# SwiGLU feed-forward on one core: six feature chunks in place of four are projected ahead of the regular loop

## Chip, core and metric

The kernel runs on one core of a Trainium2 chip. The metric is the device time of one execution in microseconds, lower is better. A run's profile gives the span between its first and last instruction, which is a little shorter than that time.

## What is computed

```python
B, S, D, F = 1, 2048, 640, 1536          # all bf16
def reference(x, w_gate, w_up, w_down):  # x [1,2048,640], w_gate, w_up [640,1536], w_down [1536,640]
    g = silu(x @ w_gate)
    u = x @ w_up
    return (g * u) @ w_down
```

## The kernel before

The 2048 rows of x are handled in four blocks of 512 (`sb`). TensorE needs x transposed, with the 640 features on partitions; `xT` holds it as five K steps (`kd`) of 128 features. The 1536 hidden features are twelve chunks of 128 (`fc`). For each block and chunk, five matmuls over `kd` accumulate the gate sum `pg` and five the up sum `pu`, each [128 features x 512 rows] of f32, that is one PSUM bank. `gate` (L210 to L217) then runs ScalarE (silu of `pg` into `sg`, L214) and VectorE (`sg` times `pu` into `aT`, L215). When a block's twelve chunks are done, the down projection runs: the last 128 output columns transposed (`po_t`, L261) and the first 512 in four groups of 128 rows (`po_a`, L291). ScalarE copies results out, SP and ACT issue the output DMAs. VectorE also computes the last four rows of the hidden layer by dot products (`row_dots`, L147) beside the matmuls, on transposed copies of the weights.

PSUM has eight banks, handed out by tag: "gu" has four, "po_a" two, "po_b" two. In the regular loop `pg` and `pu` of a chunk both come from "gu".

The first block starts differently, since nothing is loaded yet. The order of DMA issues sets what arrives when:

- the first 128 rows of x on SP's queue, the next 128 on ACT's (L86);
- five slices of the gate weights, one for each K step, 128 partitions x `EARLY` x 128 columns, by turns on SP's queue (K steps 0, 2, 4) and ACT's (1, 3) (L115);
- on SP, the crossbar copy `turn_x`, which brings rows 256 to 511 of x into `xT` transposed by the DMA engines (L105);
- on SP, the up weights of the early chunks two chunks at a time, then gate and up weights of the rest by `W_CHUNKS` (L83), then w_down (L125), the next block's crossbar copy, the broadcast rows and the transposed weights.

The order of SP's instructions is pinned at the end (`keep_order`, L314). A DMA issue waits until the DMA that used its semaphore last, eight DMAs earlier, has landed.

`head` (L219) is TensorE's work at the start. It issues 18 matmuls on a tile of ones (`warm`, L176), whose sums are not used; then it transposes the first 256 rows of x on TensorE into PSUM tiles `pt`, two K steps in a "po_a" bank that ScalarE copies to `xT` and three in a "po_b" bank that VectorE copies (L185, L190). Then come the gate sums of `EARLY` chunks side by side, K step by K step: K step 0 in two pieces of 128 rows, K steps 1 to 4 for the first 256 rows, then all five for the second 256 rows, which need the crossbar copy. Only then come the up sums of these chunks one after the other, with `gate` behind each. PE's and ACT's order is pinned as written (L241, L242). The loop at L245 skips the chunks that `head` has done.

Of the kernel before, what the change touches and what calls it, by code (L numbers as in the profile page):

```python
# [10 lines left out]
def _body(  # L11
# [9 lines left out]
    P = nc.NUM_PARTITIONS  # L21
    f32 = mybir.dt.float32
# [12 lines left out]
    S_BLK = 512  # L35
# [6 lines left out]
    T = 4  # L42
    WT_STEP = 4
    ROW_J = 0
    EARLY = 4
    W_CHUNKS = [(4, 8), (8, 12)]
    assert D % P == 0 and F % P == 0 and S % S_BLK == 0 and D > DA and SUB == 4

    consts = ctx.enter_context(tc.tile_pool(name="consts", bufs=1))
# [2 lines left out]
    psum = ctx.enter_context(  # L52
        tc.tile_pool(name="psum", bufs=2, space=bass.MemoryType.PSUM)
    )
# [24 lines left out]
    def wslice(a, b):  # L79
        return slice(a * P, b * P)  # L80

    def load_w(eng, dst, src, a, b):
        eng.dma_start(out=dst[:, :, wslice(a, b)], in_=src[:, :, wslice(a, b)])  # L83
# [14 lines left out]
    def keep_order(engine):  # L98

        traced = [i for i in nc.cur_bb.bb.instructions if i.engine == engine]  # L100
        for a, b in zip(traced, traced[1:]):
            issue_order(a, b)
# [10 lines left out]
    for kd in range(KD):  # L113
        eng = (nc.sync, nc.scalar)[kd % 2]
        eng.dma_start(  # L115
            out=wg_sb[:, kd, wslice(0, EARLY)], in_=wg_v[:, kd, wslice(0, EARLY)]
        )
    turn_x(HALF, S_BLK)
    nc.scalar.activation(silu_first[:], ones[:, 0:1], ACT.Silu)  # L119
    for a in range(0, EARLY, 2):  # L120
        load_w(nc.sync, wu_sb, wu_v, a, a + 2)
    for a, b in W_CHUNKS:
        load_w(nc.sync, wg_sb, wg_v, a, b)
# [50 lines left out]
    def warm(n):  # L174
        for _ in range(n):
            nc.tensor.matmul(  # L176
                pw[:, 0:P], lhsT=ones[:], rhs=ones[:], start=True, stop=True
            )

    def transpose_chunk(c, parts):  # L180
        c_sl = slice(c * P, (c + 1) * P)
        for copy, tag, k0, k1 in parts:
            pt = psum.tile([P, k1 - k0, P], bf16, tag=tag, name="pt")
            for kd in range(k0, k1):
                nc.tensor.transpose(  # L185
                    out=pt[:, kd - k0, :],
                    in_=x_sb[:, c, kd * P : (kd + 1) * P],
                    identity=ident[:],
                )
            copy(out=xT[:, k0:k1, c_sl], in_=pt[:])  # L190

    def proj_step(ps, w_sb, fc, sb, c0, c1, kd):
        nc.tensor.matmul(  # L193
            ps[:, c0:c1],
            lhsT=w_sb[:, kd, fc * P : (fc + 1) * P],
            rhs=xT[:, kd, sb * S_BLK + c0 : sb * S_BLK + c1],
            start=(kd == 0 and c0 in (0, HALF)),
            stop=(kd == KD - 1),
        )

    def proj(ps, w_sb, fc, sb, c0, c1):
        for kd in range(KD):
            proj_step(ps, w_sb, fc, sb, c0, c1, kd)

    def gu_tiles():
        pg = psum.tile([P, S_BLK], f32, tag="gu", name="pg", bufs=4)
        pu = psum.tile([P, S_BLK], f32, tag="gu", name="pu", bufs=4)
        return pg, pu

    def gate(pg, pu, sb, fc, n_s):  # L210

        s0 = sb * S_BLK
        sg = work.tile([P, S_BLK], f32, name="sg")
        nc.scalar.activation(sg[:, 0:n_s], pg[:, 0:n_s], ACT.Silu)  # L214
        nc.vector.tensor_tensor(  # L215
            out=aT[:, fc, s0 : s0 + n_s], in0=sg[:, 0:n_s], in1=pu[:, 0:n_s], op=ALU.mult
        )  # L217

    def head():  # L219
        dve, act = nc.vector.tensor_copy, nc.scalar.copy  # L220
        split = [(act, "po_a", 0, 2), (dve, "po_b", 2, KD)]
        pgs = [
            psum.tile([P, S_BLK], f32, tag="gu", name="pg", bufs=4)
            for _ in range(EARLY)
        ]
        warm(N_WARM)
        for c in range(HALF // P):
            transpose_chunk(c, split)

        steps = [(0, 0, P), (0, P, HALF)]  # L230
        steps += [(kd, 0, HALF) for kd in range(1, KD)]
        steps += [(kd, HALF, S_BLK) for kd in range(KD)]
        for kd, c0, c1 in steps:
            for fc in range(EARLY):
                proj_step(pgs[fc], wg_sb, fc, 0, c0, c1, kd)

        for fc in range(EARLY):
            pu = psum.tile([P, S_BLK], f32, tag=("po_a", "po_b")[fc % 2], name="pu")
            proj(pu, wu_sb, fc, 0, 0, S_BLK)
            gate(pgs[fc], pu, 0, fc, S_BLK)  # L240
        keep_order(mybir.EngineType.PE)  # L241
        keep_order(mybir.EngineType.Activation)  # L242

    head()
    for sb in range(NSB):  # L245
        n_s = S_BLK if sb < NSB - 1 else S_BLK - T
        for fc in range(KF):
            if sb == 0 and fc < EARLY:
                continue
            pg, pu = gu_tiles()  # L250
# [134 lines left out]
def kernel(tc, *args):  # L385
    _body(tc, *args)
    tc.close()
    tc.compile()
    _trim(tc.nc)
# [30 lines left out]
```

## Time and profile before

| | |
|---|---|
| median of three runs | 163.66 us (163.44 to 163.76) |
| the profiled execution, and its span | 163.73 us, 162.4 us |
| TensorE (PE) busy | 159.4 us, 98% of the span |
| VectorE (DVE), ScalarE (ACT) busy | 111.1 us, 42.6 us |
| DMA moved | 15.86 MB |
| gate matmuls (L193, `pg`) | 60.1 us |
| up matmuls (L193, `pu`) | 59.0 us |
| down projection (L291, L261) | 42.4 us and 10.3 us |

PE is the matmul unit, PEld its weight loads, which run beside it; SPq and ACTq are DMA issues from the SP and ACT queues. A group's line gives engine, operation, output and input tiles, shapes and count, then busy time, mean ns of one, and the idle time of the engine ahead of it with what ended it. A matmul's duration contains its drain, which overlaps the next one; the distance between two starts is what a stream of them costs. A DMA's time runs from issue to landing. Some matmul records are missing from the trace.

### The profile page before, as it was taken

How to read it: one execution, taken by the hardware profiler on the slowest of the kernel's cores; microseconds unless marked ns; L12 is line 12 of the kernel's file. 1: busy time of each engine (PE TensorE's matmuls, PEld its weight loads, DVE VectorE, ACT ScalarE, POOL GpSimd, SP SyncE). 2: the span in 40 equal slices, each digit the busy share in tenths (PEclk: the TensorE clock that was granted, in tenths of full speed). 3: DMA queues.
4: the chain of work that ended last, by engine and by line, in shares of the span. 5: the costliest groups of instructions: out<-in, count | busy, mean ns of one | idle time of the engine just before them, and what ended most of it. 6: DMA issues, size and time to landing. Idle time of an engine off the chain costs nothing.

```text
span 162.4 us, 2129 instructions
## 1 busy us (share of the span) xinstructions
PE 159.4 (98%) x796; PEld 78.0 (48%) x808; DVE 111.1 (68%) x250; ACT 42.6 (26%) x74; POOL 0.6 (0%) x6
## 2 busy tenths in 40 slices
PE   8999999999999999999999999999999999999995
PEld 8754444444444444444444444444444444445454
DVE  1024333499559999979919999979964999993101
ACT  5051222112232222221222322221214222222121
POOL 1000000000000000000000000000000000000000
PEclk9999999999999999999999999999999999999999
DMA  7999999995169997003110000000421000000212
GB/s 215 259 339 350 362 184 250 228 231 88 53 125 178 217 176 145 4 0 34 65 65 0 0 4 2 0 0 0 65 67 34 0 0 0 0 0 4 44 45 73
DMA packets 41961, 15.86 MB, mean 98 GB/s; under 512 B 33504, under 2 KB 41824, under 8 KB 41952
## 3 DMA queue, kind: packets, MB, share of 16 engines
q1 hardware_dynamic: 33440, 14.80, 38.0%
q10 hardware_dynamic: 8512, 0.94, 3.9%
q8 instruction: 6, 0.10, 0.3%
q14 instruction: 3, 0.02, 0.1%
HBM read 6.88 MB, written 2.62 MB: 59 GB/s over the span
## 4 chain that ended last, share of the span: by engine, by line
PE 97%; DMA 2%; issue 0%; DVE 0%
PE pg L193 32%; PE pu L193 32%; PE po_a L291 26%; PE po_t L261 6%; DMA x_sb<-in_x_dram 2%; PE pt L185 1%; DVE ot_b L302 0%
## 5 line engine op out<-in xcount | busy, mean ns | idle before, releaser
L193 PE MATMUL pg<-xT,wg_sb 128*128 128x512 bf16 (+3 forms) x258 | 60.1, 366 | 0.3
L193 PE MATMUL pu<-xT,wu_sb 128*128 128x512 bf16 (+1 forms) x239 | 59.0, 379 | 0.1
L215 DVE TENSOR_TENSOR aT<-sg,pu 128x512 bf16<-128x512 f32 (+1 forms) x48 | 32.8, 683 | 32.9 <-PE pu L193 32.9
L214 ACT ACTIVATE sg<-pg 128x512 f32<-128x512 f32 (+1 forms) x48 | 28.4, 596 | 71.5 <-PE pg L193 67.7
L291 PE MATMUL po_a<-wd_sb,aT 128*128 128x512 bf16 (+4 forms) x224 | 42.4, 348 | 0.2
L147 DVE SCALAR_TENSOR_TENSOR prod<-wgT,x_row 128x640 f32<-128x640 bf16 x48 | 39.4, 821 | 1.1
L147 DVE SCALAR_TENSOR_TENSOR prod<-wuT,x_row 128x640 f32<-128x640 bf16 x48 | 39.4, 822 | 1.0
L193 PEld LDWEIGHTS <-wg_sb 128*128 128x128 bf16 x264 | 26.3, 101 | 26.8 <-DMA wg_sb<-in_w_gate_dram 0.2
L193 PEld LDWEIGHTS <-wu_sb 128*128 128x128 bf16 x240 | 23.5, 98 | 28.0
L291 PEld LDWEIGHTS <-aT 128*128 128x128 bf16 x228 | 20.8, 98 | 21.7
L300 ACT CAST ot<-po_a 128x512 bf16<-128x512 f32 (+2 forms) x17 | 9.5, 560 | 31.8 <-PE po_a L291 20.6
L261 PE MATMUL po_t<-aT,wd_sb 128*128 128x512 bf16 (+1 forms) x47 | 10.3, 365 | 0.1
L261 PEld LDWEIGHTS <-wd_sb 128*128 128x128 bf16 x48 | 4.7, 98 | 5.1
L302 DVE CAST ot_b<-po_a 128x96 bf16<-128x96 f32 (+1 forms) x2 | 0.5, 242 | 9.7 <-PE po_a L291 9.6
L270 ACT CAST ot_t<-po_t 128x512 bf16<-128x512 f32 (+1 forms) x4 | 2.2, 560 | 11.6 <-PE po_t L261 11.6
L147 DVE DVE_READ_ACCUMULATOR prod<-wuT,x_row 128x1 f32 x48 | 3.9, 82 | 0.0
L147 DVE DVE_READ_ACCUMULATOR prod<-wgT,x_row 128x1 f32 x48 | 3.9, 82 | 0.0
L272 DVE STREAM_TRANSPOSE ot_q<-ot_t 128x512 bf16<-128x512 bf16 (+1 forms) x4 | 2.7, 678 | 1.7 <-ACT ot_t L270 1.7
L190 DVE COPY xT<-pt 128x384 bf16<-128x384 bf16 x2 | 0.7, 358 | 3.2 <-PE pt L185 3.2
L176 PE MATMUL pw<-ones 128*128 128x128 bf16 x18 | 2.1, 312 | 0.4 <-DVE ones L109 0.4
L176 PEld LDWEIGHTS <-ones 128*128 128x128 bf16 x18 | 1.8, 146 | 0.4 <-DVE ones L109 0.4
L119 ACT ACT_TABLE_LOAD x1 | 1.3, 1283 | 1.5 <-issue 1.5
(13 smaller groups left out, 4.7 us busy)
## 6 DMA issues: line engine op xcount, KB each, us to landing
wd_sb<-in_w_down_dram SPq DMA_DIRECT2D x1, 1920.0 KB, 14.2
out_dram<-ot SPq DMA_DIRECT2D x15, 128.0 KB, 1.7
wg_sb<-in_w_gate_dram SPq DMA_DIRECT2D x2, 640.0 KB, 8.3
wu_sb<-in_w_up_dram SPq DMA_DIRECT2D x2, 640.0 KB, 8.9
wu_sb<-in_w_up_dram SPq DMA_DIRECT2D x2, 320.0 KB, 5.4
x_row<-in_x_dram SPq DMA_DIRECT2D x1, 640.0 KB, 4.8
wg_sb<-in_w_gate_dram SPq DMA_DIRECT2D x3, 128.0 KB, 3.9
out_dram<-ot_q ACTq DMA_DIRECT2D x12, 32.0 KB, 2.0
```

The lines of the kernel that those rows point to most:

```text
L119: nc.scalar.activation(silu_first[:], ones[:, 0:1], ACT.Silu)
L147: nc.vector.scalar_tensor_tensor(out=prod[:], in0=wT[:, fc, :], scalar=1.0, in1=x_row[:, t, :], op0=ALU.mult, op1=ALU.mult, accum_out=acc[ ...
L176: nc.tensor.matmul(pw[:, 0:P], lhsT=ones[:], rhs=ones[:], start=True, stop=True)
L185: nc.tensor.transpose(out=pt[:, kd - k0, :], in_=x_sb[:, c, kd * P : (kd + 1) * P], identity=ident[:],)
L193: nc.tensor.matmul(ps[:, c0:c1], lhsT=w_sb[:, kd, fc * P : (fc + 1) * P], rhs=xT[:, kd, sb * S_BLK + c0 : sb * S_BLK + c1], start=(kd == 0 ...
L214: nc.scalar.activation(sg[:, 0:n_s], pg[:, 0:n_s], ACT.Silu)
L215: nc.vector.tensor_tensor(out=aT[:, fc, s0 : s0 + n_s], in0=sg[:, 0:n_s], in1=pu[:, 0:n_s], op=ALU.mult)
L261: nc.tensor.matmul(po_t[:], lhsT=wd_sb[:, kf, DA:D], rhs=aT[:, kf, sb * S_BLK : sb * S_BLK + n_t], start=(kf == 0), stop=(kf == KF - 1),)
L270: nc.scalar.copy(ot_t[:], po_t[:])
L272: nc.vector.transpose(out=ot_q[:], in_=ot_t[:])
L291: nc.tensor.matmul(po[:], lhsT=aT[:, kf, s0 : s0 + P], rhs=wd_sb[:, kf, c0:c1], start=(kf == 0), stop=(kf == KF - 1),)
L300: nc.scalar.copy(ot[:], po[:])
```

## The change

`EARLY` becomes 6. The five gate slices ahead of the crossbar copy have 768 columns (192 KB) in place of 512 (128 KB). Three loads of up weights of two chunks each follow it in place of two, and the remaining six chunks are loaded three at a time in place of four. The gate sums of the early chunks take six banks: four of "gu" and the two of "po_a", allocated once the transposes have used these. The early up sums have the two banks of "po_b" in place of taking "po_a" and "po_b" by turns.

```diff
-    EARLY = 4
-    W_CHUNKS = [(4, 8), (8, 12)]
+    EARLY = 6
+    W_CHUNKS = [(6, 9), (9, 12)]
...
         pgs = [
-            psum.tile([P, S_BLK], f32, tag="gu", name="pg", bufs=4)
-            for _ in range(EARLY)
+            psum.tile([P, S_BLK], f32, tag="gu", name="pg", bufs=4) for _ in range(4)
         ]
         warm(N_WARM)
         for c in range(HALF // P):
             transpose_chunk(c, split)
+        pgs += [
+            psum.tile([P, S_BLK], f32, tag="po_a", name="pg") for _ in range(4, EARLY)
+        ]
...
         for fc in range(EARLY):
-            pu = psum.tile([P, S_BLK], f32, tag=("po_a", "po_b")[fc % 2], name="pu")
+            pu = psum.tile([P, S_BLK], f32, tag="po_b", name="pu")
             proj(pu, wu_sb, fc, 0, 0, S_BLK)
             gate(pgs[fc], pu, 0, fc, S_BLK)
```

## The prediction

> **What bounds the kernel now.** The page's first part and its two strips come first.
>
> ```profile
> span 162.4 us, 2129 instructions
> PE 159.4 (98%) x796; PEld 78.0 (48%) x808; DVE 111.1 (68%) x250; ACT 42.6 (26%) x74; POOL 0.6 (0%) x6
> ...
> PE   8999999999999999999999999999999999999995
> ...
> PE pg L193 32%; PE pu L193 32%; PE po_a L291 26%; PE po_t L261 6%; DMA x_sb<-in_x_dram 2%; PE pt L185 1%; DVE ot_b L302 0%
> ```
>
> PE is busy in every slice but the first and the last, and the chain is PE almost alone. A dense stretch cannot be shortened by reordering it: 216 ns separate the starts of two 512-column matmuls, and the change leaves the number of streamed columns as it is. What can move is the head. Second view: busy time by stretches of the first 14 us (stretch, length, then PE busy).
>
> ```profile
> 2.30:2.64 0.34, 0.20 (x2) 0.00 (x1) 0.00 (x0) 0.34 (x1) 0.00 (x0) 1.00 1.18 357
> 2.64:3.68 1.04, 1.04 (x10) 1.04 (x11) 0.29 (x1) 0.81 (x4) 0.00 (x0) 1.00 0.96 318
> 3.68:4.54 0.86, 0.86 (x10) 0.79 (x8) 0.43 (x2) 0.30 (x1) 0.00 (x0) 1.00 1.06 302
> 4.54:4.63 0.09, 0.09 (x2) 0.00 (x1) 0.00 (x0) 0.00 (x0) 0.00 (x0) 1.00 1.56 307
> 4.63:6.30 1.67, 1.67 (x10) 1.19 (x9) 0.00 (x0) 0.00 (x0) 0.00 (x0) 1.00 1.24 234
> 7.22:9.40 2.18, 2.18 (x22) 1.95 (x20) 0.00 (x0) 0.12 (x1) 0.00 (x0) 1.00 1.09 307
> ```
>
> PE starts the x transposes at 2.64, the gate matmuls at 3.68. In 4.54 to 4.63 it starts nothing new (the 0.09 "busy" is the drain of earlier matmuls): the second gate slice is late, as the timeline says.
>
> ```profile
> 3.58 0.90 PEld L193 LDWEIGHTS <-wg_sb 128*128 128x128 bf16 x8
> 4.63 0.13 PEld L193 LDWEIGHTS <-wg_sb 128*128 128x128 bf16 x2 [0.15 <-DMA wg_sb<-in_w_gate_dram]
> ```
>
> Third, the same form of matmul, grouped by form, in 4.64 to 6.0 and in 6.6 to 7.2:
>
> ```profile
> L193 PE MATMUL pg<-xT,wg_sb 128*128 128x256 bf16 x7 | 1.7, 417 | 0.0
> ...
> L193 PE MATMUL pg<-xT,wg_sb 128*128 128x256 bf16 x8 | 1.1, 277 | 0.0
> ```
>
> By their starts they are 213 ns apart until 6.3 us and 109 ns apart from 6.5 on. So PE runs at **half rate until about 6.3**, though PEclk in the page reads full throughout. From 6.5 to its last matmul at 160.4 PE has no gap that is not a missing record (each odd gap is one 216 ns start). Hence the end is set by three things: how long PE idles before 6.3, when the full rate starts, and the column count. DVE, ACT and the tail after 160.4 follow.
>
> Fourth, DMA issues with their time to landing, in the windows 0.5 to 0.6 and 1.8 to 1.9.
>
> ```profile
> wg_sb<-in_w_gate_dram SPq DMA_DIRECT2D x1, 128.0 KB, 2.9
> wg_sb<-in_w_gate_dram ACTq DMA_DIRECT2D x1, 128.0 KB, 4.0
> ...
> wg_sb<-in_w_gate_dram SPq DMA_DIRECT2D x1, 128.0 KB, 4.0
> xT<-in_x_dram SPq DMA_TRANSPOSE x1, 4.8
> ```
>
> With the issue starts (0.46, 0.55, 0.91, 1.03, 1.39, 1.86) the five gate slices kd0 to kd4 land at 3.3, 4.6, 4.8, 5.2 and 5.4, the crossbar copy at 6.7. PE asks for them at 3.58, 4.53, 5.25, 6.10, 6.68 and 7.22. Only kd1 is late; the crossbar copy is 0.5 us early.
>
> **The change, part by part.** *Columns.* Per K step, the gates of chunks 4 and 5 become two 256-column matmuls for one of 512 (at kd0 one 256 is two of 128). At half rate they cost the same (2 x 213 = 427), at full rate 2 x 109 - 216 = 2 ns more; ten pairs: **+0.02 us**. The same columns that were computed later are gone there.
>
> *Slices of 192 KB.* Each gate slice grows by 64 KB (65.5 kB), five by 328 kB. The table above moves 302 to 318 GB/s up to 4.54 and 234 after.
> kd0: 65.5 kB take 0.21 us alone and 0.41 beside as much of kd1 on ACT's queue, so it lands at 3.5 to 3.7. PE asks at 3.58, and a landing took 0.04 us to start PE (4.59 to 4.63): a wait of 0 to 0.2.
> kd1: PE now has 12 matmuls of 128 columns before it, at 107 ns, 3.68 + 1.28 = 4.96. Ahead of its landing are 131 kB more (its own and kd0's) or 197 kB (with kd2's, which runs beside it): 0.43 to 0.65 us at 302 GB/s, 0.84 at 234. It lands at 5.0 to 5.4, and PE starts on it at 5.1 to 5.5. All idle time up to there, kd0's included, is 0.1 to 0.5 us, where it was 0.1. If the longer rows of 1536 bytes move faster, kd1 may land by 4.9 and the 0.1 is gone. So the bounds are -0.1 and +0.4 us of idle time; I take **+0.17**, between the two middle figures less 0.1 (0.11 and 0.22), because most of this traffic flows in the 302 to 318 stretches.
> kd2 (about 5.6), kd3 (6.1) and kd4 (6.5) are asked for at 6.4 and after: no wait.
>
> *What an idle 0.1 us costs.* If the full rate starts at 6.3 whatever happens, PE loses half-rate time and the cost is half: 0.08. If the start moves with the idle time it is all: 0.17. With the 0.02 that is **+0.1 to +0.2**.
>
> *The crossbar copy* stands behind the slices on SP's queue: 328 kB at 302 or 234 GB/s are 1.1 to 1.4 us, so it lands at 7.8 to 8.1. PE now reaches the second half after the rest of kd1 (to about 6.5) and 18 matmuls at 109 ns: 8.5. Hidden with 0.4 us or more, as before; where the gate starts the full rate later, PE comes later still. The up weights land about 1.4 us later (8.7 becomes 10.1) and are asked for 2.2 us later (9.3, plus two gates of 1.08, is 11.5): hidden. Chunk 6's gate weights are asked for at 11.5 + 6 x 1.08 = 18; the same number of bytes, gate and up weights of eight chunks, had landed by 13.6 (issued at 5.70, 7.9 to landing), and those of all twelve by 18.5: hidden. SP issues one DMA more (about 0.5 to 1 us, from the 0.53 and 0.84 of its neighbours), ahead of a long queue; nothing waits for it. wd, the transposed weights and x_row follow with the same total of bytes.
>
> *PSUM.* Gate sums 4 and 5 take the banks of ACT's two x copies. These end at 3.44 and 3.98 (3.07 and 3.60, each 0.37 long); the fifth and sixth matmul start at 3.68 + 4 x 0.107 = 4.11 and 4.21: free. The up sums now share two banks where they had four, so up sum n + 2 waits for the multiplication of n:
>
> ```profile
> 9.40 3.40 PE L193 MATMUL pu<-xT,wu_sb 128*128 128x512 bf16 x14
> 10.76 0.69 DVE L215 TENSOR_TENSOR aT<-sg,pu 128x512 bf16<-128x512 f32 x1 [6.48 <-PE pu L193]
> ```
>
> The first up sum starts at 9.40, its product ends at 11.45, and with 0.05 for the release (the first LDWEIGHTS of the run came 0.05 after DVE's memset) PE is free at 11.50; the third up sum starts at 9.40 + 10 x 0.216 = 11.56. **0.06 us of cover**, four times. If the product came 0.1 us later, each wait would be 0.04 and all six chunks behind PE would shift by some 0.1 in all. Cost: 0, bounds 0 and 0.2. ACT's silus run ahead, limited by the three sg buffers as now (ACT waited 0.63 for DVE once, with the next product 2 us away).
>
> **Sum.** 0.02 + 0.08 to 0.17 + 0 = +0.1 to +0.2. The profiled execution took 163.73 us, 162.4 of span and 1.3 around it; it lies 0.07 above the median of 163.66. I forecast **163.85**, against the median.
>
> **The rivals.**
> *B, the full rate comes much later (slower).* PE was busy from 0.40 to 2.30 without reaching it, idled 0.35, and then needed 2.64 to 6.3, 3.7 us, with a hole of 0.09 inside. If a hole of 0.2 or more starts that count anew, as the 0.35 may have done, then a wait at kd0 alone puts it at 3.85 + 3.7 = 7.5, one at kd1 at 5.2 + 3.7 = 8.9. That is 1.2 to 2.6 us more at half rate, half of it lost: +0.6 to +1.3, **164.3 to 165.0**. It decides once the hole passes something between 0.09 and 0.35 us. For it: the two spells above. Against: one hole of 0.09 did no harm.
> [...]
> *C, no wait at all.* The longer rows move faster and kd1 is in time: -0.1 of idle plus 0.02, **163.55 to 163.65**. For it: 12 matmuls of cover in place of 8. Against: kd1's slowest landing came 1.3 us after kd0's, in traffic that only grows.
> *D, faster.* The hole at 4.54 held the full rate back, and without it the rate starts 0.7 us or more earlier: -0.35 or more, **163.3** and below. For it: the largest price in the head is the 2.64 to 6.3 at half rate, 1.8 us lost. Against: needs C first, and the count after 2.64 can hardly be shorter than the spell of 1.9 us that did not reach it.
> *E, two banks for the up sums bind:* +0.1 to 0.2, **163.75 to 163.85** alone; it hides inside the forecast and has no chance of its own.
>
> **How the numbers follow.** The forecast's case 0.50, B 0.28, C 0.10, D 0.12. About 0.2%, 0.33 us, is what a measurement of this kernel can tell from no change, that is 163.33 to 163.99. The forecast's case holds 163.6 to 164.3 (idle up to +0.4 at full price, a bank wait on top): 0.32 of it within the bound, 0.18 above. C is within, B above, D below. Faster 0.12, same 0.42, slower 0.46. The range is 163.4 to 165.0: all of the forecast's case and C, most of B.
>
> **What would show it.** Waits of LDWEIGHTS on wg_sb in the head: one or two, 0.1 to 0.5 us in all. The 256-column matmuls turn from 417 to about 275 ns: at 6.3 to 6.6 the forecast holds, after 7.3 it is B, before 5.6 D. A wait of PE on the crossbar copy, or of a pu matmul on DVE, would show two of my zeros wrong. If PE has a gap after 12 us, the reading that only the head can move is wrong.

## The result and the profile after

The changed kernel took 164.12 us (median of 22 runs, 163.26 to 164.98), the kernel before 163.53 us (22 runs, 162.99 to 163.82) in the same series: a ratio of 1.0043 with a 95% interval of 1.0029 to 1.0058. The forecast was 163.85 against a median of 163.66, that is +0.19; measured is +0.59, inside the range, on the slower side, and from a place that the forecast had put at zero. The profiled execution of the changed kernel took 164.98 us, the longest of its runs, so what follows shows a larger loss than the median run has.

The page of the changed kernel, first part, chain and two groups (the last two columns of a group: busy time with mean ns, and idle time ahead of it with what ended it):

```profile
span 163.7 us, 2152 instructions
PE 159.2 (97%) x808; PEld 78.9 (48%) x820; DVE 111.1 (68%) x250; ACT 42.5 (26%) x74; POOL 0.6 (0%) x6
...
PE   8999999996999999999999999999999999999995
...
PE 74%; SPq 15%; DMA 5%; DVE 2%; ACTq 2%; issue 1%; ACT 0%; DVEq 0%
...
L293 PE MATMUL po_a<-wd_sb,aT 128*128 128x512 bf16 (+4 forms) x224 | 42.6, 348 | 1.6 <-ACT ot L302 1.4
...
L147 DVE SCALAR_TENSOR_TENSOR prod<-wgT,x_row 128x640 f32<-128x640 bf16 x48 | 39.4, 822 | 2.6 <-DMA wgT<-in_w_gate_dram 1.5
```

PE's strip has a 6 in its tenth slice (36.8 to 40.9 us), in the middle of what was a solid row of nines. The chain, which was PE to 97%, now has 15% of DMA issues on SP and 5% of DMA in it. The two groups name both ends of the new wait: the down projection `po_a` waits 1.4 us for ScalarE's copy `ot`, and VectorE's dot products wait 1.5 us for the transposed gate weights `wgT`. What lies between them shows in the timeline. VectorE of before, 31 to 36 us, and then of after (start, length):

```profile
31.86 0.82 DVE L147 SCALAR_TENSOR_TENSOR prod<-wgT,x_row 128x640 f32<-128x640 bf16 x1
...
34.40 0.71 DVE L272 STREAM_TRANSPOSE ot_q<-ot_t 128x512 bf16<-128x512 bf16 x1
```
```profile
33.15 0.83 DVE L147 SCALAR_TENSOR_TENSOR prod<-wgT,x_row 128x640 f32<-128x640 bf16 x1 [1.48 <-DMA wgT<-in_w_gate_dram]
...
35.63 0.71 DVE L274 STREAM_TRANSPOSE ot_q<-ot_t 128x512 bf16<-128x512 bf16 x1
```

ScalarE, 33 to 41 us, before and after:

```profile
35.14 2.04 ACTq L274 DMA_DIRECT2D out_dram<-ot_q  x4
37.23 0.59 ACT L300 CAST ot<-po_a 128x512 bf16<-128x512 f32 x1 [2.86 <-DVE prod L147]
```
```profile
36.37 2.98 ACTq L276 DMA_DIRECT2D out_dram<-ot_q  x4
39.40 1.07 ACT L302 CAST ot<-po_a 128x512 bf16<-128x512 f32 x2 [5.31 <-DVE prod L147]
```

And PE, 30 to 41 us, before and after:

```profile
33.58 7.72 PE L291 MATMUL po_a<-wd_sb,aT 128*128 128x512 bf16 x35
```
```profile
33.30 5.34 PE L293 MATMUL po_a<-wd_sb,aT 128*128 128x512 bf16 x23
40.03 1.24 PE L293 MATMUL po_a<-wd_sb,aT 128*128 128x512 bf16 x5 [1.39 <-ACT ot L302]
```

Read downwards, it is one queue behind another. VectorE worked in the written order (the third dot product starts at 34.88, the transposition at 35.63): three dot products stand ahead of the transposition `ot_q` of block 0's last 128 output columns, and they start 1.29 us later (33.15 against 31.86). The transposition is 1.23 us later. ScalarE's four output DMAs of `ot_q` wait for it and take 0.94 us longer to issue (one of the four takes 1.50 us). Behind them on ScalarE stands the copy of the first output group: 39.40 against 37.23, 2.17 us later. The groups have two PSUM banks, so PE's third group needs that copy's end. Before, the copy ended at 37.82 and PE came at 38.76: 0.95 us to spare. Now it ends at 39.98 and PE could have started at 38.48: a hole of 1.55 us. Two things make the copy late, 1.23 us of transposition and 0.94 us of slow issue. Without the slow issue, these figures give as an estimate a hole of some 0.6 us and an end some 0.3 us later than before.

The sum closes. PE's last matmul starts 1.27 us later (161.62 against 160.35): the hole of 1.55 less 0.28, since PE reached the down projection of block 0 earlier than before (33.30 against 33.58). The head, on which the forecast turned, had gained in this execution.

Why are the gate weights late? Their load stands behind all other loads on SP's queue, so it shows what these lose. The last up weights land at 18.45 before and 18.84 after, w_down at 23.72 and 24.15, the broadcast rows at 28.80 and 29.73, the first transposed gate weights at 31.65 and 33.05. The issues at 24 us with their time to landing, before and after:

```profile
x_row<-in_x_dram SPq DMA_DIRECT2D x1, 640.0 KB, 4.8
wgT<-in_w_gate_dram SPq DMA_TRANSPOSE x1, 7.0
```
```profile
x_row<-in_x_dram SPq DMA_DIRECT2D x1, 640.0 KB, 5.3
wgT<-in_w_gate_dram SPq DMA_TRANSPOSE x1, 8.0
```

So 0.43 of the 1.40 us are there when w_down lands; the rest is added behind it, by loads that the change leaves as they were, and why is not shown. This pair is not typical in that. Over five profiles with the loads of before and five with the new ones, w_down is on average 0.83 us later (23.25 and 24.08) and the first transposed gate weights 1.17 us (31.31 and 32.48): most of the lateness comes ahead of w_down.

The DMA rate from 10 to 18 us (last column, GB/s; ahead of it the busy share of the DMA engines, over 1 where packets overlap) before and after:

```profile
10.00:18.00 8.00, 8.00 (x38) 3.63 (x37) 3.44 (x5) 2.65 (x5) 0.00 (x0) 1.00 1.09 353
```
```profile
10.00:18.00 8.00, 7.95 (x45) 4.21 (x44) 3.44 (x5) 3.37 (x6) 0.00 (x0) 1.00 1.10 327
```

In that stretch the rows are mostly 1024 bytes before (512 columns of a weight) and 768 after (384 columns), at its start 512 (256 columns). The engines are busy all the time in both, so the queue does not run dry; each packet brings less.

### The profile page after: what moved, and what is told of

Read it like the earlier page. It is cut to its first block, busy times and chain, and to the rows that moved or that the text cites. A ratio compares the mean times of both kernels' runs of the same rounds, so it can differ in the third digit from the quotient of the medians.

```text
span 163.7 us, 2152 instructions
## 1 busy us (share of the span) xinstructions
PE 159.2 (97%) x808; PEld 78.9 (48%) x820; DVE 111.1 (68%) x250; ACT 42.5 (26%) x74; POOL 0.6 (0%) x6
## 3 DMA queue, kind: packets, MB, share of 16 engines
q10 hardware_dynamic: 8512, 1.07, 4.1%
## 4 chain that ended last, share of the span: by engine, by line
PE 74%; SPq 15%; DMA 5%; DVE 2%; ACTq 2%; issue 1%; ACT 0%; DVEq 0%
PE pu L193 24%; PE pg L193 24%; PE po_a L293 23%; SPq L105 8%; DMA wgT<-in_w_gate_dram 5%; SPq L83 4%; PE po_t L263 4%; ACTq L276 2%; DVE prod L147 2%; SPq L125 1%; SPq L115 1%; DVE ot_q L274 0%; ACT ot L302 0%; SPq L136 0%; SPq L86 0%
## 5 line engine op out<-in xcount | busy, mean ns | idle before, releaser
L193 PE MATMUL pg<-xT,wg_sb 128*128 128x512 bf16 (+3 forms) x270 | 59.5, 356 | 0.3
L193 PEld LDWEIGHTS <-wg_sb 128*128 128x128 bf16 x276 | 27.2, 101 | 25.6 <-DMA wg_sb<-in_w_gate_dram 0.2
```

The source lines that it names most:

```text
L193: nc.tensor.matmul(ps[:, c0:c1], lhsT=w_sb[:, kd, fc * P : (fc + 1) * P], rhs=xT[:, kd, sb * S_BLK + c0 : sb * S_BLK + c1], start=(kd == 0 ...
```

## The experiments

Theory T: the time is lost at 38 us, through the late transposed weights and the dots ahead of the transposition ("late dots"). Rival R, the forecast's own: it is lost in the head, by waits on the larger slices and by a later full rate. All ratios are against runs of the kernel before on the same chip, with 95% intervals.

**A second profile of the changed kernel.** No edit.

> The changed kernel once more, for a second profile. In its first profile TensorE stands still from 38.5 to 40.0 us, ahead of the third output group of block 0, and the full matmul rate starts at 5.55 us. Theory T (late dots): the first transposed gate weights land about 1.4 us later than before, VectorE's three dot products ahead of the transposition of the block's last columns wait for them, ScalarE's output DMAs stand behind that and its copies behind these. By T the hole is there again, 0.3 to 1.6 us, with the landing after 32.2 us, and the time is 0.4 to 0.8 us over before. Rival R (head): the hole was an accident of that execution and the loss comes from waits on the gate slices and from the moment of the full rate: then there is no hole at 38 us here, and the head alone explains the time.

Measured: 164.59 us (163.48 to 165.92) against 163.33, ratio 1.0077 (1.0053 to 1.0101). Its profiled execution, 165.92 us, the longest of its twelve, has no hole at 38 us, and the transposed gate weights landed at 32.09, not after 32.2; the median is 1.26 us over before, not 0.4 to 0.8. T's expectation failed here, and this execution is as R has it. It has another hole. Timeline from 4.6 us, and the 256-column matmuls by form in 6.5 to 9.7 and in 10 to 12:

```profile
4.67 0.13 PEld L193 LDWEIGHTS <-wg_sb 128*128 128x128 bf16 x2 [1.12 <-DMA wg_sb<-in_w_gate_dram]
```
```profile
L193 PE MATMUL pg<-xT,wg_sb 128*128 128x256 bf16 x17 | 3.8, 421 | 0.0
```
```profile
L193 PE MATMUL pg<-xT,wg_sb 128*128 128x256 bf16 x20 | 2.4, 276 | 0.0
```

The first gate slice landed at 4.63 us. The trace tells its landing in sixteen shares: fifteen had landed by 3.54, one was 1.1 us behind. PE started nothing new for 1.06 us, and the full rate came only at 9.9 us. PE itself reached the down projection at 35.78, 2.5 us later than in the first profile, so the late copy did not hold it (it ended at 40.52, and its bank was needed at 40.97): the two losses do not add, the later of two chains sets the end.

**The dots later.**

```diff
-        do_dots(3)
+        if sb > 0:
+            do_dots(3)
         nc.vector.transpose(out=ot_q[:], in_=ot_t[:])
```

> The changed kernel without the three dot products that VectorE makes ahead of the transposition of block 0's last columns; they are made later, among the others. By T nothing of VectorE stands ahead of that transposition any more, the hole at 38 us is gone and the time falls by 0.4 to 0.8 us, to that of before or a little under it (ratio 0.996 to 1.001). By R it stays at 1.003 to 1.006.

Measured in the same series as the run above: 163.18 us, ratio 1.0008 (0.9984 to 1.0032). That is 1.4 us less than the changed kernel in that series. ScalarE's queue in 33 to 41 us:

```profile
35.11 3.25 ACTq L277 DMA_DIRECT2D out_dram<-ot_q  x4
38.40 1.11 ACT L303 CAST ot<-po_a 128x512 bf16<-128x512 f32 x2 [4.07 <-DVE prod L147]
```

The DMAs are issued at 35.11 as before, although the gate weights land as late as 32.0. A hole of 0.31 us is left: one of the four issues took 1.6 us here too. One of the twelve runs took 165.19; the others lie between 162.91 and 163.99. T holds; the loss is gone although the slow issue is still there.

**The broadcast rows and the gate weights ahead of the next block's crossbar copy.** The same hole, closed from the other side, with VectorE's order untouched.

```diff
-    turn_x(S_BLK, 2 * S_BLK)
     nc.sync.dma_start(out=x_row[:], ...)
     turn_w(wgT, wgt_v)
+    turn_x(S_BLK, 2 * S_BLK)
```

> The changed kernel with the next block's crossbar copy of x moved behind the broadcast rows and the transposed gate weights on SP's queue; VectorE's order is that of the changed kernel. The copy took about 2.2 us, so the first transposed gate weights land about 2 us earlier, near 30 us. By T the hole at 38 us goes by this as well, and the time falls to that of the changed kernel with late dots (ratio to before 0.998 to 1.002). By R, which puts the loss into the head, it stays at 1.003 to 1.008.

Measured: 163.32 us against 163.50, ratio 0.9992 (0.9978 to 1.0006). The first transposed gate weights land at 28.5 us. ScalarE again:

```profile
35.15 2.00 ACTq L276 DMA_DIRECT2D out_dram<-ot_q  x4
37.20 0.59 ACT L302 CAST ot<-po_a 128x512 bf16<-128x512 f32 x1 [2.82 <-DVE prod L147]
```

These starts are those of before to within 0.03 us, and PE has no hole after the head. T holds by a second route.

**Longer rows.** The same bytes in nearly the same order, in four loads where there were seven.

```diff
-    W_CHUNKS = [(6, 9), (9, 12)]
+    W_CHUNKS = [(6, 12)]
...
-    for a in range(0, EARLY, 2):
-        load_w(nc.sync, wu_sb, wu_v, a, a + 2)
+    for a, b in [(0, 2), (2, EARLY)]:
+        load_w(nc.sync, wu_sb, wu_v, a, b)
```

> The changed kernel with the same bytes in the same order, but the weights behind the crossbar copy in longer rows: up weights of chunks 2 to 5 in one load (1024 bytes a row, were 512), gate and up weights of chunks 6 to 11 in one load each (1536 bytes, were 768). In the traces the loads of the changed kernel after the crossbar copy run at about 264 GB/s to the last up weight where before reached about 336, which gives away some 0.9 us, and the transposed gate weights come that much later. If the short rows are the cause, these land 0.6 to 1.0 us earlier (31 to 31.6 us in place of 32 to 33), most of the hole at 38 us is gone and the ratio to before is 0.998 to 1.003. If it is only the 320 KB more ahead of the crossbar copy, the landing stays at 32 to 33 us and the ratio at 1.003 to 1.008.

Measured: 163.43 us against 163.45, ratio 1.0004 (0.9988 to 1.0021), with one run of twelve at 166.07. The rate from 10 to 18 us:

```profile
10.00:18.00 8.00, 8.00 (x44) 4.10 (x42) 3.72 (x6) 3.37 (x6) 0.00 (x0) 1.00 1.07 369
```

369 GB/s against 327; the first transposed gate weights land at 31.2, as in the kernel before, and a hole of 0.25 us is left at 38 us. So most of the lateness came from the short rows, not from the 320 KB that moved ahead of the crossbar copy: these are still ahead of it here. The edit also makes three loads fewer, and no run parts the two; for the rows speaks that the DMA engines were busy throughout in all three (share 1.09, 1.10 and 1.07), and that all profiles agree: 350 to 356 GB/s in six with the loads of before, 321 to 330 in six with the new ones, 368 and 369 in two with long rows. The 264 and 336 GB/s of the expectation do not come out of the landings: from the crossbar copy's landing to that of the last up weight it is 271 GB/s after (2.95 MB in 10.87 us) and 278 before (3.28 MB in 11.77 us).

**The loads alone,** under the old order of matmuls, and **the same with the dots later.**

```diff
     EARLY = 4
-    W_CHUNKS = [(4, 8), (8, 12)]
+    LOADED = 6
+    W_CHUNKS = [(6, 9), (9, 12)]
...
-            out=wg_sb[:, kd, wslice(0, EARLY)], in_=wg_v[:, kd, wslice(0, EARLY)]
+            out=wg_sb[:, kd, wslice(0, LOADED)], in_=wg_v[:, kd, wslice(0, LOADED)]
...
-    for a in range(0, EARLY, 2):
+    for a in range(0, LOADED, 2):
```

> The loads of the changed kernel (gate slices of 768 columns, three loads of up weights by two chunks, the rest by three) under the matmul order of before (four chunks early). By T the landing of the transposed gate weights moves as in the changed kernel, because it hangs on the loads: a hole at 38 us of 0.3 us or more, or a time 0.3 to 0.8 us over before. In addition TensorE has only 8 matmuls ahead of the second gate slice and waits up to 0.5 us in the head. By R the head's waits alone cost 0.1 to 0.3 us and there is no hole at 38 us.

> The new loads under the old matmul order, and the three dot products of block 0 made later. The loads alone cost 1.3 us. Its profile had a wait of 1.0 us for the first gate slice and the full rate only at 9.8 us, but the unprofiled runs also lie 0.7 to 1.5 us over before. T alone: the loss is that of the dots, and the ratio falls to 1.000 to 1.002. R alone: it is the wait for the large slices and what it does to the moment of the full rate, and the ratio stays at 1.006 to 1.010. If both matter and the later chain sets the end, it lies between, at 1.002 to 1.006, with a wide spread.

Measured: 164.64 us, ratio 1.0100 (1.0065 to 1.0135), and with the dots later 164.15 us, ratio 1.0050 (1.0032 to 1.0068), from six runs each, in different series. The transposed gate weights land late here too (33.01 and 32.25), as T has it. But the first of the two profiles has no hole at 38 us: the first slice was 0.96 us late, the full rate came at 9.7 us, and PE came to the third output group 1.0 us after ScalarE's copy had ended. T's expectation failed for it. Read as the difference of the two ratios, half of the loads' loss would be the dots; as the intervals touch and no profile shows a hole, that is not shown. The other half, which stays with the dots later, is the head: with 8 matmuls ahead of the second slice in place of 12, PE waited 1.3 us in all in the head of the one and 1.9 us in that of the other. With six chunks the added matmuls cover most of what the larger slices cost; with four they do not.

**Two banks for the up sums alone.**

```diff
-            pu = psum.tile([P, S_BLK], f32, tag=("po_a", "po_b")[fc % 2], name="pu")
+            pu = psum.tile([P, S_BLK], f32, tag="po_b", name="pu")
```

> The kernel before with the early up sums in the two banks of po_b alone, as in the changed kernel. T and R both say no difference (ratio 0.998 to 1.002). If two banks bind, the early up sums start late and the time is 0.1 to 0.2 us over before.

Measured: 163.38 us against 163.33, ratio 0.9998 (0.9985 to 1.0011). No loss, and no wait of PE on VectorE in the early up sums, in this profile or in those of the changed kernel.

**The kernel before with each repair, and once more unchanged.** The edits are those above.

> The kernel before with the three dot products of block 0 made later. In its profile ScalarE's copy had 0.95 us to spare ahead of the third output group, so T says no hole and no difference where the full rate starts at 6 us, and a gain where it starts early, because TensorE then comes up to 0.7 us sooner and the dots are what is late: ratio 0.996 to 1.000. R says no difference, 0.999 to 1.001.

> The kernel before with the transposed gate weights ahead of the next block's crossbar copy. TensorE had 0.95 us to spare there and making the dots late brought nothing, so T says no difference, 0.998 to 1.001. Beside the changed kernel with the same move it shows what six early chunks are worth by themselves: equal if the head is worth nothing either way.

> The kernel before once more, for a second profile. [...] The time is the same as before (0.998 to 1.002).

Measured: dots later 163.36 us, ratio 0.9998 (0.9984 to 1.0012); gate weights first 163.56 us, 1.0004 (0.9988 to 1.0019); unchanged 163.51 us, 1.0004 (0.9993 to 1.0016). The kernel before had enough to spare; the small gain that T allowed it is not there. With the gate weights first, six early chunks (0.9992) and four (1.0004) cannot be told apart. In the second profile of the unchanged kernel the full rate starts at 4.3 us, in the first at 6.3. The 256-column matmuls there in 4.3 to 6.0 us:

```profile
L193 PE MATMUL pg<-xT,wg_sb 128*128 128x256 bf16 x14 | 1.8, 274 | 0.0
```

There PE then stood 0.46 us for the crossbar copy, which landed at 6.67. The same wait is in the two other profiles of this group, 0.36 and 0.45 us, where the full rate came at 3.8 and 3.9. So part of what an early full rate gains is lost again in the kernel before; the changed kernel and its repaired forms, with more matmuls ahead of the copy, do not wait for it in any of their six profiles.

**Both repairs together** on the changed kernel.

> Both repairs on the changed kernel: long rows, and the transposed gate weights ahead of the next block's crossbar copy. If the dots of block 0 were all that cost, this is the kernel with transposed weights first, ratio 0.997 to 1.001: the long rows then hide. By R it is no better than the changed kernel, 1.003 to 1.008.

Measured: 163.51 us against 163.45, ratio 0.9999 (0.9982 to 1.0017). No version beat the kernel before by more than its interval.

**A longer hole in the head of the kernel before.**

```diff
-    N_WARM = 18
+    N_WARM = 8
```

> The kernel before with 8 warm-up matmuls in place of 18, so that TensorE idles from about 1.2 to 2.6 us instead of from 2.3. The profiles so far have the full rate at 3.8 to 6.4 us where no hole in the stretch ahead was over 0.5 us, and at 9.7 and 9.9 us where one of about 1 us lay at 3.5. [...] If only the sum of busy time counts, it starts at most 1.1 us later: 1.001 to 1.003.

Measured: 164.12 us, ratio 1.0039 (1.0021 to 1.0056), above the 1.001 to 1.003 of the sum of busy time, though the interval reaches into them. The profile, of the longest run, goes against that sum too: PE waits 1.6 us for x, and the 256-column matmuls are still slow in 5.5 to 8.5 us (418 ns).

```profile
PEld L185 <- DMA x_sb<-in_x_dram: 1.6, 1, 1.6
```
```profile
L193 PE MATMUL pg<-xT,wg_sb 128*128 128x256 bf16 x16 | 3.6, 418 | 0.0
```

The full rate came at 8.6 us. By the sum of busy time it would have been 7.5 at the latest (6.4, the latest without a long hole, plus the 1.1 of ten matmuls).

## Why the prediction was right and where it was wrong

*What bounds the kernel:* PE, and from the end of the head on it had no hole before. "If PE has a gap after 12 us, the reading that only the head can move is wrong": it has one, of 1.55 us. The strip showed that PE was dense; it could not show with how little to spare. The 0.95 us of cover ahead of block 0's third output group were in the trace of before (copy ended at 37.82, bank needed at 38.76), and the prediction did not read it.

*The step that failed:* "wd, the transposed weights and x_row follow with the same total of bytes", at a cost of zero. The bytes are the same, their rate is not: 327 GB/s with the shorter rows against 353, and what is last in the queue collects the loss. In the profiles the first transposed gate weights land at 30.9 to 31.7 us with the loads of before (five executions) and at 32.0 to 33.1 with the new ones (five). The second omission was to follow "nothing waits for it" only to SP's own work: VectorE waits for the weights (1.48 us in the first profile), in order, and ScalarE and PE stand behind VectorE.

*Columns (+0.02) and PSUM (0):* held. The two banks cost nothing (ratio 0.9998).

*The slices (+0.17 of idle time):* neither right nor wrong in the mean. In the first profile the first two slices were in time (landings at 3.57 and 4.43, asked for at 3.65 and 4.93) and the third, which the prediction had in time, was 0.10 us late, because PE came to it sooner at the full rate (from 5.55 us); with long rows, where the full rate came at 3.8, it was 0.70 us late. In the second the first slice was 1.06 us late, beyond my bound of 0.5 for all waits, through one share of sixteen. The slower landing was priced from the mean rate; what PE waits for is the last share. The landing of the second slice, 4.59, from which the forecast counted, is also the latest of the six profiles with slices of 128 KB (3.64 to 4.59).

*The crossbar copy and the up weights:* hidden, as forecast; the copy landed at 7.97, forecast 7.8 to 8.1. "As before" was true of the one profile that the prediction had: with an earlier full rate the kernel before waits for the copy.

*Price of an idle 0.1 us, and rivals B and D:* the moment of the full rate does not hang on the work alone. The same kernel had it at 6.3 and at 4.3. In the profiles whose holes up to that moment were at most 0.53 us each it lies between 3.8 and 6.4 (eleven executions of ten kernels), and in the three with a hole of 0.96 to 1.5 us at 8.6 to 9.9. So B exists: it made the second profile of the changed kernel the slowest of its series. B's mechanism was half wrong. Its limit for the hole, 0.09 to 0.35 us, was too low: in the changed kernel with the gate weights first a hole of 0.47 us ended at 3.92, and the full rate came at 6.1 us, where a new count of 3.7 us would give 7.6. A count that starts anew after the hole would have given 4.68 + 3.7 = 8.4 in the second profile; it was 9.9. In the three profiles with the long hole the full rate came 5.2, 5.3 and 5.9 us after the hole's end. What sets the moment (the prediction has it as "where the gate starts the full rate later") no run shows. The runs scatter more than the first three did: 22 runs of the kernel before span 0.83 us, the three 0.32.

*C:* its condition, no wait on the first two slices, was met in the first profile, and the head did come out ahead by 0.28 us, mostly by the earlier full rate.

So the sign and the range were right, the size was a third of the measured one, and the term that made the difference was put at zero. That the sign came out is luck: it was forecast from a slower head, and the medians lose by late dots. The size itself is not steady: +0.59 us in the first series, +1.26 in the second. With the hole at 38 us closed, or all but closed, by any of three ways the changed kernel equals the one before (0.9992 to 1.0008): the head, on which the forecast turned, is worth nothing that these runs can tell, apart from single runs (165.19 and 166.07 in two of the repaired kernels), about as slow as that of the second profile; what they lost to is not shown.

*Open:* why one share of a slice lands 1.1 us after the others; and why one of ScalarE's four DMA issues at 36 us takes 1.07 to 1.68 us in some executions and at most 0.7 in others. It is slow in five of the six profiles of kernels with six early chunks, and in none of the eight with four, so it may belong to the change; no run tests that. Of the repaired kernels, the one with the gate weights first is without it; the other three keep it, and it leaves holes of 0.22 to 0.31 us.

## What to carry to other kernels

When a change alters the rows of early loads, follow the queue to its last load and ask who waits for that one, engine by engine, even 30 us later: an engine off the critical path can stand ahead of one that is on it, as VectorE's late dots here stood ahead of PE's hole of 1.55 us. Beside the wait list, look for cover that is nearly used up: for each buffer that the bounding engine needs, when it came free and when it was needed. And price a wait for a load by its last share (here once 1.1 us behind the other fifteen), not by the mean rate.

## What the runs showed of the hardware

- Rows of mostly 1536, mostly 1024 and mostly 768 bytes moved 369, 353 and 327 GB/s in the same stretch of the same queue. Against the rows of mostly 1024 bytes that is 0.93 for 768 and 1.05 for 1536, in a stretch that holds other rows too.
- The full matmul rate started anywhere from 3.8 to 6.4 us in kernels without a long hole, by estimate worth up to 1.3 us of the span (half the difference: in the kernel before, 256-column matmuls start 213 ns apart ahead of it and 109 ns behind it), while the profile's granted clock read full (1.00) throughout.
- A hole of 0.92 us (new loads with dots later) or 0.86 us (gate weights first in the kernel before) after the full rate had started did not end it.
